# Joined score stretches, no copied left keys, no warm-up zeros, and a new written order in a fused attention and MLP kernel

## The chip, the cores and the metric

The kernel runs on one core of one Trainium2 chip. The metric is the device time of one execution in microseconds; a table below gives the runs of the kernel before. In the text PE is TensorE, DVE is VectorE, ACT is ScalarE, POOL is GpSimd and SP is SyncE, as in the profile.

## The reference

Banded attention with a linear bias by distance, and a squared-ReLU MLP on its output:

```
B, H, S, D = 4, 8, 768, 64         # d_model = 512, d_ff = 2048
scores = q @ k.T / sqrt(D)
keep   = (key < 8) or (0 <= query - key < 96)
scores = where(keep, scores - slope[h] * dist, -1e9)   # dist is 96 for a far global key
x   = softmax(scores) @ v          # rearranged to 3072 tokens x 512
h   = relu(x @ w_in)
out = (h * h) @ w_out              # fp32, 3072 x 512
```

## The kernel before

The 3072 tokens are 24 tiles of 128 rows (`j` = 0 to 23, six to a batch entry); two tiles make a block (`blk` = 0 to 11). A query of a tile sees only the keys of its own tile and of the one before, and the eight global keys; those are copied into the first eight columns of the left tile's keys and values (`gk`, `gv`). The first tile of a batch entry has no left tile and half the scores.

For a tile the steps are: `tr` and `T` (q and k transposed on PE and copied from PSUM) for tiles 0 to 7, or one DMA transpose `T` on SP from tile 8 on; `bias` (tiles 0 to 2 alone, a matmul that adds the bias); `sc` (the scores, matmuls of 64 rows, into two or four PSUM banks); `exp` on ACT, one for each bank; `mul` on DVE (by a table of the exponentiated bias and mask, from tile 3 on); `pv` on PE in two halves; `norm` on DVE (reciprocal and product); and `trx` with `xT` on PE and ACT or DVE, or `xT` by a DMA transpose from tile 8 on.

The MLP of block 0 is plain: `s1`, `relu`, `sq`, then `s2`, `o` and `st`. From block 1 (second layer) and block 2 (first layer) on it takes seven products in place of eight, in Strassen's manner: sums of inputs (`xs`), seven products `h` in three banks x, y and z, with the partial sums carried out of PSUM by `u` and added by `c`, squares `q`; then sums of the hidden values (`sum`), seven products `s2...p1` to `p7`, parts carried out by `part`, results `o` and stores `st`. `isum` and `wsum` make the sums of the two weight matrices once.

Nothing is scheduled at build time: `ORDER` is a written list of steps, and the instructions of all engines are issued in that order. A word names a step; `@A`, `@V` or `@P` after it puts it on ACT, DVE or POOL; digits after a colon are the PSUM banks, of eight, that the step opens; `#2` is the second step of the same name. Each engine runs its own steps in this order and waits for the data, the banks and the buffers that they need:

```
for word in ORDER.split():
    word, _, banks = word.partition(":")
    name, _, letter = word.partition("@")
    ...
    o["banks"] = [int(b) for b in banks]
```

The planner's costs, due times and dependences (`key`, `deps`, `takes`, `LEADS`, `SAFE`) are still in the code but issue nothing. The first loads (`ld.q.1`, `ld.win.3.0` and so on) and later ones (`load.j`: v, q and k of a tile) go through POOL's queue one after the other; q and k of tile 0, the DMA transposes and the stores go through SP's queue. Ahead of everything PE runs eight matmuls on zeros (L372), and between the transposes of q and of k of tile 0 a second eight (`warm`, L532).

For tiles 14, 15, 19, 20 and 22 (`COPY`), the keys that the next tile uses as its left keys are copied out whole, with the global keys, to a buffer `kl`; for the others `gk` writes the global keys in place after the tile's own scores. `JOIN` names tiles whose scores are emitted in the same step as those of the tile before; it is empty. In block 11 the last product `p3` is done in two cuts of 192 and 64 columns.

Of the kernel before, what the change touches and what calls it, by code (L numbers as in the profile page):

```python
# [57 lines left out]
tr.0.0:0 warm:7 tr.1.0:1 T.1.0@V bias.0.0:23 T.0.0@A sc.0.0 ld.win.3.0 exp.0.0.0 ld.k.1 tr.1.1:4 bias.1.0:5670 T.1.1@V ld.q.1  # L58
tr.0.1:1 ld.v.0 exp.0.1.0 T.0.1@V sc.1.0 exp.1.0.1 pv.0.0:2 ld.q.2 tr.0.2:3 norm.0.0 ld.k.2 T.0.2@V ld.k.3 exp.1.1.1
pv.0.1:4 tr.1.2:1 bias.2.0:7203 ld.v.1 norm.0.1 exp.1.1.0 ld.q.3 tr.1.3:6 gk.1@A T.1.2@A sc.2.0 exp.1.0.0 T.1.3@V  # L60
ld.k.4 pv.1.0:4 ld.v.2 gk.2@V exp.2.1.0 exp.2.1.1 norm.1.0 trx.0:1 xT.0@A ones.6 pv.1.1:5 tr.0.3:6 T.0.3@V exp.2.0.0
tr.1.4:2 ld.win.6.0 sc.3.0:4361 ld.q.4 norm.1.1 ld.v.3 trx.1:7 gv.1@V exp.2.0.1 exp.3.0.0 pv.2.0:5 exp.3.1.0 exp.3.0.1
T.1.4@V xT.1@V pv.2.1:0 ld.k.5 ld.win.2.0 exp.3.1.1 gk.3@A ld.win.2.1 norm.2.0 s1.0.3:2 mul.3.0 s1.0.6:4 ld.win.4.0
tr.0.4:7 ld.q.5 ld.v.4 norm.2.1 mul.3.1 relu.0.6@A s1.0.3#2 gv.2@P pv.3.0:3 norm.3.0 trx.2:5 T.0.4@A pv.3.1:6
ld.win.1.0 norm.3.1 ld.win.0.1 xT.2@A sc.4.0:1047 exp.4.1.1 exp.4.1.0 tr.1.5:3 T.1.5@A s1.0.2:5 trx.3:6 xT.3@V
ld.win.0.0 ld.win.5.0 s1.0.2#2 s1.0.2#3 s1.0.2#4 relu.0.3@V exp.4.0.1 ld.v.5 gv.3@P exp.4.0.0 gk.4@V sq.0.6@V
relu.0.2@A s1.1.3:7 ld.win.7.0 relu.1.3@A load.6 s1.1.6:0 mul.4.1 tr.0.5:6 mul.4.0 sq.0.3@V s1.1.2:3 T.0.5@A ld.wout.3
pv.4.0:2 ld.wout.1 sq.0.2@V sc.5.0:4157 ld.wout.0 s1.0.4:6 relu.1.2@A exp.5.1.1 s1.0.1:3 sq.1.3@A exp.5.0.0 relu.0.4@V
s1.1.4:7 ld.wout.2 norm.4.0 pv.4.1:4 gv.4@P norm.4.1 sq.0.4@A load.7 exp.5.1.0 sq.1.2@A relu.1.4@A s1.0.0:6 gate.9
ld.wout.4 mul.5.0 s1.0.0#2 sq.1.4@A s1.0.0#3 s1.1.5:2 trx.4:1 exp.5.0.1 relu.1.6@V s1.1.1:4 ld.wout.5 s1.0.1#2  # L70
relu.1.1@A E0.1 mul.5.1 relu.1.5@A pv.5.0:7 s1.1.7:0 s1.1.0:5 sq.1.1@V norm.5.0 ld.wout.6 E0.0 sq.1.5@V tr.1.6:4
sq.1.6@A pv.5.1:2 relu.1.7@A tr.0.6:7 s1.0.0#4 norm.5.1 xT.4@A sq.1.7@A h.2.0.p2:0 ld.wout.7 T.1.6@V h.2.1.p2:1
trx.5:2 xT.5@V relu.1.0@A sq.1.0@A gate.14 h.2.0.p1:5 xs.2.0 s1.0.5:4 sum.1.2 s1.0.7:2 relu.0.1@A xs.2.1 gate.10
sum.1.0 sum.1.1 relu.0.0@A T.0.6@A sc.6.0:36 wsum.0.0 sum.1.3 sq.0.0@A sq.0.1@A s2.0.0.0:7 relu.0.7@A s2.0.1.0 load.9
exp.6.0.0 xs.2.2 s2.0.2.0 exp.6.1.0 s2.0.3.0 s2.0.0.1:2 s2.0.1.1 wsum.2.0 relu.0.5@A sq.0.7@A s2.0.2.1 load.8 mul.6.0
wsum.1.0 s2.0.3.1 tr.0.7:3 tr.1.7:6 gate.15 isum.0.0 h.2.1.p1:4 T.0.7@A s2.0.4.0 isum.0.1 s2.1.p1.0:3 isum.3.1 T.1.7@A
sq.0.5@A pv.6.0:6 isum.1.1 s2.0.4.1 s2.0.5.1 u.2.0.1@A c.2.0.c11 s2.0.5.0 gate.11 u.2.1.1@A h.2.1.p6 q.2.0.c11@A
isum.1.0 T.8 s2.0.6.1 u.2.1.2@A s2.0.6.0 isum.3.0 pv.6.1:0 h.2.0.p6 wsum.2.1 wsum.0.1 s2.1.p1.1 s2.0.7.1 c.2.1.c11
norm.6.0 gate.13 o.0.1@V st.0.1 s2.0.7.0 h.2.1.p7 part.1.p1@A s2.1.p6.0 u.2.0.2@A o.0.0@A u.2.1.3@A h.2.0.p7 h.2.1.p4
T.9 norm.6.1 wsum.3.0 u.2.0.3@A sc.7.0:1762 c.2.1.c21@A wsum.1.1 h.2.1.p5:0 c.2.1.c22 q.2.1.c11@A s2.1.p2.0:4  # L80
exp.7.1.0 exp.7.0.0 isum.2.1 load.10 h.2.0.p4 exp.7.0.1 mul.7.0 exp.7.1.1 s2.1.p2.1 isum.2.0 s2.2.p1.0:7 q.2.1.c21@A
mul.7.1 h.2.0.p5:1 s2.1.p6.1 part.1.p6@A trx.6:6 gate.12 c.2.0.c21@A load.12 pv.7.0:2 xT.6@A c.2.0.c22 q.2.1.c22@A
q.2.0.c22@A s2.2.p1.1 h.2.1.p3 s2.1.p7.0 wsum.3.1 o.1.p2 norm.7.0 h.2.0.p3 pv.7.1:5 s2.1.p7.1 q.2.0.c21@A st.0.0
c.2.1.c12 s2.1.p5.0 s2.1.p5.1 part.1.p7@A q.2.1.c12@A s2.1.p4.0 T.10 s2.1.p4.1 c.2.0.c12 gk.7@V q.2.0.c12@A o.1.p5
o.1.p4@A sc.8.0:6201 st.1.1 part.2.p1@A s2.1.p3.0 norm.7.1 sum.2.0 sum.2.1 s2.1.p3.1 trx.7:5 xT.7@V o.1.p3 h.3.0.p1:3
exp.8.1.0 gk.8@V h.3.1.p1:2 exp.8.0.0 exp.8.1.1 exp.8.0.1 h.3.0.p2:6 xs.3.0 u.3.1.1@A sc.9.0:1540 s2.2.p6.0 mul.8.0
xs.3.1 mul.8.1 u.3.0.1@A h.3.0.p6 exp.9.0.1 exp.9.1.1 gv.7@V h.3.1.p2:4 c.3.0.c11 h.3.1.p6 c.3.1.c11 exp.9.0.0
pv.8.0:0 s2.2.p6.1 pv.8.1:6 load.11 norm.8.0 u.3.1.2@A s2.2.p2.0:1 sum.2.2 gv.8@P q.3.1.c11@A norm.8.1 xT.8 h.3.1.p7
h.3.0.p5:4 u.3.0.2@A h.3.0.p7 s2.2.p2.1 exp.9.1.0 st.1.0 part.2.p6@A xs.3.2 u.3.1.3@A q.3.0.c11@A h.3.1.p5:0 s2.2.p7.0
u.3.0.3@A mul.9.1 mul.9.0 s2.2.p7.1 c.3.1.c22 T.12 c.3.0.c22 pv.9.0:6 h.3.1.p3 o.2.p2 h.3.0.p4 c.3.1.c12 load.15  # L90
norm.9.0 q.3.1.c22@A h.3.0.p3 s2.3.p1.0:5 s2.3.p1.1 c.3.0.c12 q.3.0.c22@A pv.9.1:0 c.3.0.c21@A part.2.p7@A norm.9.1
q.3.1.c12@A h.3.1.p4 q.3.0.c12@A h.4.0.p1:3 c.3.1.c21@A s2.2.p5.0 part.3.p1@A gk.9@V sc.10.0:6402 s2.2.p5.1
q.3.0.c21@A sum.3.0 sum.3.1 s2.2.p4.0 s2.2.p4.1 exp.10.1.0 sum.2.3 exp.10.0.0 exp.10.0.1 h.4.0.p2:4 T.11 u.4.0.1@A
exp.10.1.1 gk.10@V gv.9@A s2.3.p6.0 o.2.p5 mul.10.0 c.4.0.c11 xT.9 h.4.1.p1:6 o.2.p4@A mul.10.1 s2.2.p3.0 s2.2.p3.1
q.3.1.c21@A s2.3.p2.0:0 sum.3.2 u.4.1.1@A pv.10.0:2 pv.10.1:4 s2.3.p6.1 xs.4.0 gate.17 o.2.p3 part.3.p6@A xs.4.1
s2.3.p2.1 norm.10.0 h.4.0.p6 h.4.1.p6 q.4.0.c11@A gv.10@A norm.10.1 u.4.0.2@A load.13 s2.3.p7.0 sc.11.0:7124 u.4.1.2@A
sum.3.3 h.4.0.p7 h.4.1.p7 xs.4.2 exp.11.1.0 o.3.p2 exp.11.0.0 u.4.0.3@V s2.3.p7.1 sc.12.0:17 exp.11.1.1 exp.11.0.1
gate.16 xT.10 h.4.0.p4 c.4.0.c21@A mul.11.0 st.2.0 mul.11.1 h.4.1.p2:4 c.4.1.c11 exp.12.1.0 s2.3.p5.0 pv.11.0:2
pv.11.1:3 s2.3.p5.1 norm.11.0 part.3.p7@A h.4.0.p5:7 q.4.1.c11@A u.4.1.3@A norm.11.1 h.4.1.p5:4 q.4.0.c21@A gate.20
s2.3.p4.0 c.4.0.c22 load.14 s2.3.p4.1 h.4.0.p3 T.13 gate.18 load.16 c.4.1.c22 exp.12.0.0 h.4.1.p4 q.4.1.c22@A h.4.1.p3  # L100
xT.11 s2.4.p2.0:2 h.5.0.p1:3 q.4.0.c22@A o.3.p5 mul.12.0 c.4.0.c12 o.3.p4@A c.4.1.c21@A u.5.0.1@A c.4.1.c12 T.15
s2.3.p3.0 q.4.0.c12@A s2.3.p3.1 q.4.1.c12@V q.4.1.c21@A h.5.0.p2:1 o.3.p3 sc.13.0:5764 st.3.1 st.2.1 h.5.1.p1:0
exp.13.0.0 T.14 s2.4.p2.1 c.5.0.c11 exp.13.1.0 pv.12.1:1 q.5.0.c11@A s2.4.p1.0:5 xs.5.0 sum.4.0 pv.12.0:7 xs.5.1
s2.4.p1.1 mul.13.0 h.5.0.p6 gk.13@V u.5.1.1@A exp.13.0.1 h.5.1.p6 exp.13.1.1 h.5.0.p5:6 sum.4.1 norm.12.0 norm.12.1
h.5.1.p2:4 xs.5.2 mul.13.1 c.5.1.c11 h.5.1.p5:7 u.5.1.2@A sum.4.2 gate.19 part.4.p1@A h.5.1.p7 u.5.0.2@A h.5.0.p7
o.4.p2 u.5.0.3@A c.5.0.c22 pv.13.0:1 u.5.1.3@A norm.13.0 s2.4.p6.0 s2.4.p6.1 xT.12 st.3.0 q.5.1.c11@A T.16 part.4.p6@A
h.5.0.p4 pv.13.1:4 s2.4.p5.0 sum.4.3 c.5.0.c21@A h.5.0.p3 h.5.1.p4 q.5.0.c22@A s2.4.p7.0 norm.13.1 s2.4.p7.1 s2.4.p5.1
c.5.0.c12 q.5.0.c21@A kl.15@V part.4.p7@A c.5.1.c22 q.5.0.c12@A sc.14.0:1346 o.4.p5 s2.4.p4.0 xT.13 exp.14.0.1 kl.14@V
h.5.1.p3 gv.13@P q.5.1.c22@V c.5.1.c12 c.5.1.c21@A s2.4.p4.1 load.17 h.6.0.p1:4 s2.4.p3.0 s2.4.p3.1 exp.14.1.1
exp.14.1.0 exp.14.0.0 sc.15.0:0673 mul.14.1 mul.14.0 xs.6.0 o.4.p4@A xs.6.1 h.6.0.p2:1 o.4.p3 q.5.1.c12@A s2.5.p1.0:5  # L110
u.6.0.1@A c.6.0.c11 exp.15.0.0 exp.15.1.0 exp.15.1.1 sum.5.0 s2.5.p1.1 h.6.0.p6 u.6.0.2@A exp.15.0.1 sum.5.1 load.18
h.6.0.p5:2 part.5.p1@A pv.14.0:0 norm.14.0 pv.14.1:6 h.6.1.p1:1 u.6.1.1@A h.6.0.p7 gv.14@P st.4.0 s2.5.p6.0 u.6.0.3@A
# [1319 lines left out]
```

## Time and profile before

| | |
|---|---|
| runs, us | 199.13, 199.85, 200.0 (median 199.85) |
| profiled execution, us | 199.37 |
| its span, us | 197.6 |
| instructions in the span | 6777 |
| DVE busiest groups | `c` sums L995 (45 + 15), products L690 (39), norms L779 (48) |
| ACT busiest groups | squares L1015 (72), exponentials L665 (78 + 10), `u` copies L429 (42 + 15) |
| loads by POOL's queue | 24 of v, 23 each of q and k, 10 pieces of w_in, 8 of w_out |

The span runs from the first to the last instruction of the core; the execution's own time is 1.8 us longer. A group is the instructions of one line, engine and form; its mean is the time of one from start to end, and instructions of one engine overlap a little, so that the distance from start to start is shorter than that mean. A chain piece gives the time that the chain spends in a run of instructions of one line.

### The profile page before, as it was taken

To read this page: it belongs to the slowest core of one execution; us is meant where nothing else is said; L and a number is where in the kernel's file an instruction comes from. 1 tells how busy PE (TensorE), PEld (TensorE's weight loads), DVE (VectorE), ACT (ScalarE), POOL (GpSimd) and SP (SyncE) were. 2 spreads that over 40 slices of the span, in tenths; PEclk is the share of its full clock that TensorE was granted. 3 is DMA by queue.
4 is the path that set the end of the run, shared out by engine and by line. 5 is a ranking of instruction groups with operands and counts; after the bars stand their busy time and mean duration, and the time that the engine had idled before them with its cause. 6 is when DMAs were issued, how large, how long until landed. Compare 5 with 4: busy or idle time off the path is not lost.

```text
span 197.6 us, 6777 instructions
## 1 busy us (share of the span) xinstructions
PE 191.9 (97%) x2776; PEld 169.6 (86%) x2776; DVE 173.2 (88%) x423; ACT 163.0 (82%) x335; POOL 80.4 (41%) x101
## 2 busy tenths in 40 slices
...
GB/s 127 153 158 171 181 181 185 182 202 159 139 209 191 75 200 88 145 174 210 151 129 203 114 124 194 160 121 92 136 81 116 154 55 56 27 30 163 0 106 106
DMA packets 111857, 26.91 MB, mean 136 GB/s; under 512 B 103379, under 2 KB 109011, under 8 KB 111827
## 3 DMA queue, kind: packets, MB, share of 16 engines
...
q8 instruction: 21, 0.34, 0.6%
...
## 4 chain that ended last, share of the span: by engine, by line
PE 95%; DVE 2%; issue 1%; ACT 0%; DVEq 0%
PE bank L1212 35%; PE bank L950 32%; PE bank L1061 7%; PE bank L599 6%; PE bank L748 5%; PE bank L1339 4%; PE bank L372 2%; PE bank L506 2%; PE bank L532 1%; DVE qkT L433 1%; PE bank L816 1%; PE bank L579 0%; ACT qkT L429 0%; DVE o L1287 0%; DVE v L433 0%
## 5 line engine op out<-in xcount | busy, mean ns | idle before, releaser
L1015 ACT ACTIVATE hs<-hr 128x512 bf16<-128x512 f32 x72 | 44.8, 641 | 5.1 <-DVE hr L995 4.7
L665 ACT ACTIVATE esc<-bank 128x512 bf16<-128x512 f32 x78 | 42.9, 614 | 1.3 <-PE bank L599 1.0
L1212 PE MATMUL bank<-wsum,hsum 128*128 128x256 bf16 x264 | 36.2, 273 | 0.0
L1212 PEld LDWEIGHTS <-hsum 128*128 128x128 bf16 x360 | 32.1, 98 | 4.1 <-issue 0.5
L995 DVE CUSTOM_DVE_ANT_0 hr<-bank,early 128x512 f32<-128x512 f32 x45 | 30.4, 685 | 2.5 <-PE bank L950 1.5
L950 PEld LDWEIGHTS <-win 128*128 128x128 bf16 x480 | 29.7, 98 | 1.0
L950 PEld LDWEIGHTS <-qk_first 128*128 128x128 bf16 x480 | 29.7, 98 | 1.0
L429 ACT COPY early<-bank 128x512 f32<-128x512 f32 x42 | 24.5, 591 | 3.6 <-PE bank L950 3.3
L690 DVE TENSOR_TENSOR at<-esc,E 128x1024 bf16<-128x1024 bf16 x39 | 26.7, 696 | 0.1
L1212 PEld LDWEIGHTS <-hs 128*128 128x128 bf16 x264 | 24.0, 98 | 2.6
L310 POOL DMA_DIRECT2D qk<-in_q_dram x18 | 16.0, 890 | 21.9 <-DMA qkT<-qk 20.6
L1212 PE MATMUL bank<-wout,hs 128*128 128x256 bf16 x176 | 24.9, 273 | 0.0
L310 POOL DMA_DIRECT2D v<-in_v_dram x18 | 16.0, 888 | 18.3 <-DVE v L480 14.9
L950 PE MATMUL bank<-xT,win 128*128 128x128 bf16 x320 | 23.4, 219 | 0.0
L431 POOL COPY v<-v 8x520 bf16<-8x520 bf16 x8 | 5.7, 718 | 43.3 <-PE bank L748 43.3
L950 PE MATMUL bank<-xs,qk_first 128*128 128x128 bf16 x320 | 22.8, 219 | 0.0
L779 DVE TENSOR_TENSOR x<-bank,rs 128x256 bf16<-128x256 f32 x48 | 20.4, 425 | 1.7
L865 ACT ACTIVATE hr<-bank 128x512 f32<-128x512 f32 x33 | 19.4, 598 | 1.3 <-PE bank L950 0.4
L748 PE MATMUL bank<-v,at 128*128 128x65 bf16 x352 | 17.8, 193 | 0.0
L1287 DVE TENSOR_TENSOR o<-bank,part 128x256 f32<-128x256 f32 (+2 forms) x34 | 13.8, 410 | 3.3 <-PE bank L1212 3.2
L429 ACT COPY part<-bank 128x256 f32<-128x256 f32 x29 | 10.9, 375 | 7.1 <-PE bank L1212 6.9
L310 POOL DMA_DIRECT2D qk<-in_k_dram x18 | 16.1, 897 | 0.9 <-DMA win<-in_moe_w_in_dram 0.5
...
## 6 DMA issues: line engine op xcount, KB each, us to landing
out_dram<-o SPq DMA_DIRECT2D x22, 256.0 KB, 2.5
...
wout<-in_moe_w_out_dram POOLq DMA_DIRECT2D x8, 256.0 KB, 8.5
win<-in_moe_w_in_dram POOLq DMA_DIRECT2D x6, 256.0 KB, 6.9
...
```

Source lines behind the costliest of these rows:

```text
L310: nc.gpsimd.dma_start(out=dst, in_=src)
L429: nc.scalar.copy(dst, src)
L665: nc.scalar.activation(out=tiles[tag, j, g][:, odd], in_=tiles.pop(("sc", j, odd, g)).rearrange("p a c -> p (a c)"), func=Act.Exp, scale=s ...
L690: nc.vector.tensor_mul(at, tiles.pop(("esc", j, g)), bias)
L748: nc.tensor.matmul(out=po[:, hi, :], lhsT=tiles["at", j, g][:, odd, at * P : (at + 1) * P], rhs=v_sb[kj][:, h, :], start=(i == 0), stop=(i ...
L779: nc.vector.tensor_tensor(out=x[:, 4 * hf : 4 * hf + 4, :], in0=po[:, :, :D], in1=rs.to_broadcast([P, 4, D]), op=Alu.mult,)
L865: nc.scalar.activation(dst, src, Act.Relu)
L950: nc.tensor.matmul(out=tiles["h", blk, g, bank][:, n], lhsT=left_[:, s, k], rhs=right_[:, k], start=opens and n == 0 and k == 0, stop=k == ...
L995: nc.vector._custom_dve(TENSOR_ADD_SAT, out=hr, in0=src, in1=tiles.pop(("u", blk, g, i)), s0=float("inf"), s1=0.0,)
L1015: nc.scalar.activation(hs, hr, Act.Square)
L1061: nc.tensor.matmul(out=hT[:, c, cols], lhsT=w_in_sb[s][:, kt, c * P : (c + 1) * P], rhs=tiles["xT", blk][:, kt, cols], start=(kt == 0), st ...
L1212: nc.tensor.matmul(out=tiles["acc", blk, bank][:, cols], lhsT=left_[:, s], rhs=right_[:, cols], start=first and s == 0, stop=s == NSTEP - ...
```

## The change

Seven things differ; all the rest of the code is the same.

- `JOIN` holds tiles 7, 13 and 19: their scores are emitted in the step of tiles 6, 12 and 18, and that step opens six banks (`sc.6.0:751063`: the first two for tile 6, the other four for tile 7). 21 score steps are left of 24.
- `COPY` is empty: no `kl` step, five more `gk` steps.
- The second eight matmuls on zeros are gone.
- The buffers of `u` are taken from a list of free ones, not in turn.
- `pv` names the load of the left tile's values as a dependence (for the planner).
- In block 11 both cuts of `p3` are entered as done with the last matmul, and the order has both adds behind all matmuls.
- `ORDER` is new in whole. On POOL's queue q of tile 1 is now first, then k of tile 1 (before: a piece of w_in, then k, then q); the pieces of w_in and `v` of tile 5 come after most q, k and v, and tiles 6 and 7 are loaded ahead of w_out. Loads and DMA transposes stand in groups of their own.

```diff
-    JOIN = set()
-    COPY = [14, 15, 19, 20, 22]
+    JOIN = {(7,0),(13,0),(19,0)}
+    COPY = []
...
-    NKEEP = 8
...
-        if j == 0:
-            def emit_warm(e):
-                for _ in range(NKEEP):
-                    nc.tensor.matmul(out=psum(), lhsT=zero[:, :P], rhs=zero, start=True, stop=True)
-
-            plan.op(("warm",), {"PE": 0.216 * NKEEP}, emit_warm, key=base)
...
-        def open_sc(gs, j=j):
-            for n, (g, odd) in enumerate((g, odd) for g in gs for odd in range(2)):
+        def open_sc(gs, at=0, j=j):
+            for n, (g, odd) in enumerate(((g, odd) for g in gs for odd in range(2)), at):
...
-        def emit_sc(e, gs, j=j, todo=todo, open_sc=open_sc):
+        def emit_sc(e, gs, at=0, j=j, todo=todo, open_sc=open_sc):
             if isinstance(gs, list):
                 for f, gs in gs:
-                    f(e, gs)
+                    f(e, gs, at)
+                    at += 2 * len(gs)
                 return
...
-                deps.append(glob.get(("v", j - 1)))
+                deps += [glob.get(("v", j - 1)), land["v", j - 1]]
...
-    u_next = [0]
+    u_free = list(u_ring)
...
-                    u = u_ring[u_next[0] % NU]
-                    u_next[0] += 1
+                    u = u_free.pop(0)
...
+                        u_free.append(u)
...
-                for o, cols in zip(done, cuts):
+                for o, cols in zip([done[-1]] * len(cuts), cuts):
```

Of the new order, the parts that the text speaks of. The start, up to the first step of the MLP (POOL's loads and the other engines' steps stand in one list):

```
ld.q.1 ld.k.1 ld.v.0 ld.k.2 ld.q.2 ld.v.1 ld.q.3 ld.k.3 ld.q.4 ld.v.2 ld.k.4 ld.k.5 ld.v.3 ld.win.3.0 ld.q.5 ld.v.4
ld.win.0.0 ld.win.1.0 tr.0.0:0 T.0.0@V ones.6 load.6 ld.win.0.1 ld.win.2.0 ld.win.2.1 ld.v.5 ld.win.6.0 ld.win.4.0
ld.win.7.0 ld.win.5.0 load.7 ld.wout.0 ld.wout.1 ld.wout.2 ld.wout.3 ld.wout.5 ld.wout.4 ld.wout.6 ld.wout.7 tr.1.0:1
T.1.0@A bias.0.0:23 tr.0.1:4 sc.0.0 exp.0.1.0 exp.0.0.0 tr.1.1:5 T.0.1@V T.1.1@V bias.1.0:6701 sc.1.0 gate.9 gk.1@V
pv.0.0:4 norm.0.0 exp.1.0.0 pv.0.1:3 exp.1.0.1 tr.1.2:5 norm.0.1 T.1.2@V bias.2.0:2640 tr.0.2:3 exp.1.1.0 pv.1.0:7
norm.1.0 exp.1.1.1 trx.0:5 pv.1.1:1 gv.1@V norm.1.1 xT.0@V T.0.2@A sc.2.0 exp.2.1.0 exp.2.0.1 tr.0.3:3 tr.1.3:7 gk.2@A
T.0.3@V T.1.3@V exp.2.0.0 trx.1:1 tr.0.4:6 sc.3.0:5437 pv.2.0:2 exp.2.1.1 pv.2.1:0 exp.3.0.1 xT.1@V exp.3.0.0 norm.2.0
gk.3@V gv.2@V T.0.4@V tr.1.4:1 norm.2.1 T.1.4@A exp.3.1.0 mul.3.0 tr.1.5:3 sc.4.0:2516 exp.3.1.1 exp.4.0.0 trx.2:4
mul.3.1 pv.3.0:0 pv.3.1:7 exp.4.1.0 norm.3.0 norm.3.1 s1.0.3:2 exp.4.0.1 gk.4@A s1.0.3#2 trx.3:5 tr.0.5:0 exp.4.1.1
gv.3@V mul.4.0 mul.4.1 pv.4.0:1 xT.2@V pv.4.1:7
```

The joined score steps and what is ahead of them, and a stretch of block 11:

```
s2.0.0.0:3 ... s2.0.7.0 wsum.2.0 o.0.0@A st.0.0 T.11 c.2.1.c11 s2.0.4.1 sc.6.0:751063
s2.2.p4.1 o.2.p4@A h.4.1.p6 o.2.p3 xT.10 st.2.0 st.2.1 sum.3.0 u.4.1.2@A sc.12.0:304726
sc.17.0:1325 s2.4.p4.1 gate.22 load.22 sum.5.2 exp.17.0.0 exp.17.0.1 exp.17.1.1 sum.5.0
sum.5.1 o.4.p4@A s2.4.p3.1 s2.5.p1.0:1 c.6.0.c12 o.4.p3 exp.17.1.0 h.6.1.p4 mul.17.1 c.6.1.c21@A sc.18.0:205673
h.11.0.p7 s2.10.p6.0 s2.10.p6.1 q.11.0.c11@A u.11.1.2@V sum.10.3 sum.10.2 u.11.0.3@V
c.11.0.c22 part.9.p7@A h.11.1.p7 sum.9.3 s2.10.p2.1 s2.9.p4.0 o.9.p5 q.11.0.c22@A h.11.0.p3
```

And the last steps, before and after:

```
s2.11.p3.0 s2.11.p3.1 s2.11.p3.0#2 o.11.p3 s2.11.p3.1#2 st.11.0#2 o.11.p3#2 st.11.0#3      # before
s2.11.p3.0 s2.11.p3.1 ... s2.11.p3.0#2 s2.11.p3.1#2 o.11.p3 st.11.0#2 o.11.p3#2 st.11.0#3  # after
```

204 lines of the change are left out of this document (97 added, 107 removed).

## The prediction

> **What bounds the kernel now.** I read the page first: busy times, then the chain that ended last.
>
> ```profile
> span 197.6 us, 6777 instructions
> PE 191.9 (97%) x2776; PEld 169.6 (86%) x2776; DVE 173.2 (88%) x423; ACT 163.0 (82%) x335; POOL 80.4 (41%) x101
> PE 95%; DVE 2%; issue 1%; ACT 0%; DVEq 0%
> ```
>
> The chain is TensorE (PE) for 95% of the span, and VectorE (DVE) is close behind with 88% busy. So the next question is where PE waits. The list of waits has these lines for PE's matmuls, and asked for 40 to 193 us alone it has none:
>
> ```profile
> PE bank L372 <- DVE early L361: 1.2, 1, 1.2
> PE bank L599 <- DVE qkT L433: 1.1, 3, 0.5
> PE bank L1212 <- DVE o L1287: 0.5, 1, 0.5
> ```
>
> From 40 us to the last step the old order therefore keeps PE fed without one wait. A new order can gain there only by less PE work, and it loses whatever wait it brings in. The chain in order of time, and the timeline of the same place, show the one thing there that is not work:
>
> ```profile
> 18.29 1.32 PE bank L1061 x16
> 19.83 0.45 PE bank L1061 x8
> 42.55 0.45 PE bank L506 x8
> 84.21 0.49 PE bank L748 x16
> 140.69 0.55 PE bank L599 x16
> 141.24 0.55 PE bank L950 x8
> 141.79 0.44 PE bank L1212 x4
> 142.23 0.45 PE bank L950 x8
> ```
>
> ```profile
> 140.69 0.22 PE L599 MATMUL bank<-qkT,kl 64*128 64x128 bf16 x2
> 140.74 0.22 PE L599 MATMUL bank<-qkT 64*128 64x128 bf16 x2
> ```
>
> A product of eight matmuls (L950) takes 0.45, but 0.55 right behind a stretch of scores (L599). The sixteen score matmuls start in pairs 0.055 apart, 8 x 0.055 = 0.44, yet the stretch takes 0.55. So each stretch costs 0.10 going in and 0.10 coming out. The other rows give PE's prices: four transposes (L506) 0.22, a `pv` (L748) 0.25, half an `s2` step (L1212) 0.44; a matmul itself lasts 0.22 from start to end.
>
> **The change part by part.** The base is the profiled execution: 199.37 us, with a span of 197.6; the median of the runs is 199.85, and 0.5% of it, about what a measurement of this kernel can tell, is 1.0 us.
>
> *Joined stretches.* Tiles 6+7, 12+13 and 18+19 go in one stretch each, so three changes in and out go: 3 x 0.2 = -0.6.
>
> *Copies, small edits.* The five `kl` copies fall away, and five narrow `gk` copies take their place, on ACT and DVE. PE waits for neither, so this is worth 0; should it be the cover of a late step, some tenths. The free list for `u` and the planner's extra dependences add no instruction. No PE wait in the list names a key tile transposed by DMA, so keeping loads and transposes apart has nothing to give PE: 0.
>
> *Start: no zeros, loads in another order.*
>
> ```profile
> 1.19 3.60 PE L372 MATMUL bank<-early 128*128 128x512 bf16 x8 [1.19 <-DVE early L361]
> 1.25 0.56 SPq L319 DMA_DIRECT2D plain<-in_k_dram  x1
> 1.34 0.89 POOL L307 DMA_DIRECT2D win<-in_moe_w_in_dram  x1 [0.17 <-issue]
> 2.22 0.90 POOL L307 DMA_DIRECT2D qk_first<-in_k_dram  x1
> 5.43 2.62 PE L532 MATMUL bank<-early 128*128 128x512 bf16 x8
> 7.89 0.60 PE L506 MATMUL bank<-ident,plain 128*128 128x128 f32 x4
> 9.71 1.09 ACT L665 ACTIVATE at<-bank 128x512 bf16<-128x512 f32 x2 [3.44 <-PE bank L599]
> 11.62 0.23 PE L599 MATMUL bank<-qkT 64*128 64x128 bf16 x2 [0.52 <-DVE qkT L433]
> 17.31 2.12 ACT L665 ACTIVATE esc<-bank 128x512 bf16<-128x512 f32 x4
> 18.12 1.49 PE L1061 MATMUL bank<-xT,win 128*128 128x128 bf16 x16
> ```
>
> ```profile
> plain<-in_k_dram SPq DMA_DIRECT2D x1, 256.0 KB, 6.0
> win<-in_moe_w_in_dram POOLq DMA_DIRECT2D x6, 256.0 KB, 6.9
> ```
>
> The zeros (L532) end at 8.05, but k of tile 0, issued at 1.25, lands 6.0 later, at 7.25. They hide that wait and hold the next transposes up by 0.6 at most (7.89 against 7.3). The first exponentials, now at 9.71, then come 0 to 0.6 earlier; I take 0, as scores still wait for copy and bias.
>
> What is late next is the first step of the MLP, `s1.0.3`, at 18.12 now. In the new order it stands behind `pv.3.1` on PE, and thus behind all fourteen exponentials of tiles 0 to 3 on ACT. Two of them take 1.09 and four 2.12, so 0.5 each and the last about 0.6. From 9.7: 13 x 0.5, two copies `T` and a `gk` ahead (about 1.2) is 17.4; the waits for `sc.1.0` and `sc.2.0`, which no longer overlap with other work, I put at 1.1; so the last starts at 18.5 and ends at 19.1, and its `mul` (0.7, row further down) and `pv` (0.25) bring `s1.0.3` to 20.2. The weight is not sooner: `ld.win.3.0` goes from first to fourteenth on POOL's queue, 1.34 + 13 x 0.88 + 6.9 = 19.7. By 20.2 the old order has done three steps of `s1` (L1061 in the chain, 1.32 + 0.45 = 1.8 us of PE); the new one has instead the scores of tile 4, one transpose, one `trx` and one `pv` more, 1.3. Behind by 0.45. Then `pv.4.0` and `pv.4.1` stand behind `mul.4.1`, again four exponentials on, another 0.45 (0 to 0.9). Of the loads behind, `load.6` with its three DMAs goes ahead of most `win` pieces: `ld.win.0.1`, now twenty-second, lands at 1.34 + 21 x 0.88 + 6.9 = 26.7, about when PE comes to it (26.5 with the delays so far). Together +0.9, between 0 and 1.6. On SP stores go behind transposes; none frees a buffer that PE waits for.
>
> A rule of the Trainium skill bears on the zeros ("TensorE: Matmul & The Clock Gate", Part 1): the array runs at half rate until a window of about 3.4 us of activity has passed. The trace agrees: the first eight matmuls of 512 columns take 3.60, the second eight 2.62, so the rate changed within them. By the rule, PE idle from 5.4 to 7.3 could leave the start cold; the first rival below prices this.
>
> *Tail.*
>
> ```profile
> 194.16 0.36 DVE L1287 TENSOR_TENSOR o<-bank,part 128x192 f32<-128x192 f32 x1 [0.84 <-PE bank L1212]
> 194.57 0.28 PE L1212 MATMUL bank<-wout,hsum 128*128 128x64 bf16 x4 [0.45 <-DVE o L1287]
> 194.88 0.22 DVE L1287 TENSOR_TENSOR o<-bank,part 128x64 f32<-128x64 f32 x1 [0.37 <-PE bank L1212]
> ```
>
> The last matmul of the block before ends just ahead of 194.16, and PE starts 0.05 after the add ends at 194.52: such a handing on costs 0.05. The last four matmuls no longer wait 0.45 for the first add; both adds now follow all matmuls, so the first add and its store come 0.1 later and the second 0.3 earlier at best, behind the first store's issue on SP: -0.1 (-0.3 to 0.1).
>
> *What the joined stretches ask for.* A joined stretch opens six of the eight banks at once. The rows for the instructions that free them, and DVE's pace:
>
> ```profile
> L429 ACT COPY o<-bank 128x512 f32<-128x512 f32 x1 | 0.6, 585 | 0.0
> L429 ACT COPY o<-bank 128x256 f32<-128x256 f32 x10 | 3.8, 377 | 3.6 <-PE bank L1212 3.5
> L690 DVE TENSOR_TENSOR at<-esc,E 128x1024 bf16<-128x1024 bf16 x39 | 26.7, 696 | 0.1
> 46.36 0.68 DVE L888 TENSOR_TENSOR plain<-win 128x1024 bf16<-128x1024 bf16 x1
> 46.96 0.68 DVE L1132 TENSOR_TENSOR wsum<-wout 128x1024 bf16<-128x1024 bf16 x1
> 58.32 0.42 DVE L1287 TENSOR_TENSOR o<-bank,part 128x256 f32<-128x256 f32 x1
> 58.66 0.17 DVE L778 RECIPROCAL rs<-bank 128x4 f32<-128x4 f32 x1
> 58.87 0.42 DVE L779 TENSOR_TENSOR x<-bank,rs 128x256 bf16<-128x256 f32 x1
> 59.21 0.68 DVE L1167 TENSOR_TENSOR hsum<-hs 128x1024 bf16<-128x1024 bf16 x1
> ```
>
> `sc.18.0:205673` takes bank 3, which `sc.17.0` filled and `exp.17.1.0` empties. Between the two PE has three steps of `s2` and one `h`, 4 x 0.44 = 1.8. ACT has, 0.2 after the scores' end, three exponentials (1.5), `o.4.p4` (0.38 or less; 0.3), then the one wanted, 0.6: 2.6. PE stands for 0.8, more if ACT comes late: 0.9 (0.8 to 1.1). `sc.12.0:304726` takes bank 6, emptied by `o.2.p4` on ACT, whose source `s2.2.p4.1` is the last but one step on PE: 0.22 + 0.38 + 0.05 against one `h` of 0.45 is 0.2, and `exp.11.0.1` and `part.3.p1` stand ahead on ACT: 0.5 (0.2 to 0.65). `sc.6.0:751063` takes bank 3 of `s2.0.7.0`, emptied by `o.0.0`: 0.22 + 0.59 + 0.05 against `s2.0.4.1`, 0.43: 0.4 (0.2 to 0.45). Sum +1.8, between 1.2 and 2.2: the joining costs three times what it saves.
>
> *DVE from `sc.6.0` to `sc.10.0`.* With tile 7 pulled in, its products and norms meet six `wsum`. Up to and with `c.3.0.c11`, which frees bank 7 for `sc.10.0:2107`, DVE has 21 instructions of the long kind, 0.60 from start to start (46.36, 46.96): 12.6; six norms of 0.55 (58.66 to 59.21): 3.3; three `o` of 0.34: 1.0; `xs`, `gk`, gate 0.9: 17.8 in all. PE has 11 `h`, 19 `s2`, 6 `pv`, 2 `trx` and three stretches of scores: 4.9 + 8.3 + 1.2 + 0.4 + 2.3 = 17.1. DVE is late by 0.8 if it never waits itself, and it must wait for some `pv`; less what the wait at `sc.6.0` already gave: +0.9 (0.4 to 1.8).
>
> *The rest of the order.* Near the end `h.11.0.p3` waits for `c.11.0.c22`, behind `u.11.1.2`, two sums and `u.11.0.3`, now on DVE: 5 x 0.6 + 0.1 against five PE steps, 2.2: +0.8 (0 to 0.9). In all the letters move six `u`, seven `part` and three `q` from ACT to DVE, some 9 us for the engine that was already at 88%. Seven more places (`sc.15.0`, `s2.4.p2.0`, `s2.4.p3.0`, `sc.20.0`, `sc.21.0`, `pv.21.0`, `sc.23.0`) have the consumer 0.2 to 0.4 too close by the same count, 2.1 together; a delay met earlier takes up part of them, so +0.9 (0 to 2.2).
>
> Sum: -0.6 - 0.1 + 0.9 + 1.8 + 0.9 + 0.8 + 0.9 = +4.6; 199.4 + 4.6 = 204.0. With the low ends: -0.6 - 0.3 + 0 + 1.2 + 0.4 + 0 + 0 = +0.7; with the high ends -0.6 + 0.1 + 1.6 + 2.2 + 1.8 + 0.9 + 2.2 = +8.2.
>
> **The rivals.** *Cold start, 205.5.* If the array runs at half rate from 7.3 until about 11, the PE work ahead of the second tile's scores (two fp32 transposes' worth, biases, two stretches, about 3.2 us) doubles, ACT starves and `s1.0.3` slips by about 1.5. For it: the idle gap that replaces L532. Against it: the work after 7.3 is nearly dense itself. Chance 0.15.
>
> *The waits melt, 200.7.* The waits are not added but overlap: once PE is late, DVE and ACT have caught up, and only the longest counts. Then -0.7 + 0.9 from the start and 1.1 for the longest: +1.3. Against it: three of them hang on a PE step just ahead, which a delay moves along. Chance 0.15; about half of it is within 1.0 us of no change.
>
> *Faster, 197.7.* q and k of tile 1 lead the queue, so `sc.1.0`, at 11.6 now, follows 1.0 sooner, and PE keeps this lead: -0.7 - 1.0 = -1.7. It decides if `s1.0.3` starts before 19.0 and PE shows no wait past 40 us. Against it: the fourteen exponentials. Chance 0.05.
>
> *Not what it says.* On POOL's queue q of tile 1 stands before its k, against the description. Scores need both, so it moves nothing: no case of its own.
>
> **How the numbers follow.** Forecast 0.6, near 204; cold start 0.15; melted 0.15; faster 0.05; elsewhere 0.05. The range 200.7 to 206.5 leaves out the fast case, half the melted one and the top of the sum. Slower by over 0.5%: 0.6 + 0.15 + 0.08 + 0.03 = 0.86; within: 0.09; faster: 0.05.
>
> **What would show it.** PE waits at the three joined stretches named, by ACT, of 0.4 to 0.9; a wait by DVE ahead of `sc.10.0`; `s1.0.3` at about 20; score stretches down to 21; DVE busier than 173 us, ACT less than 163. It is wrong if the list of PE's waits past 40 us is again empty.

## The result, and the profile after

The changed kernel takes 202.31 us (median of four runs, 202.05 to 203.18) where the kernel before took 199.62 beside it: a ratio of 1.0147, 95% interval 1.0117 to 1.0178. It is slower by 2.7 us; the forecast of 204.0 had the side right and was 1.7 too high. Ratios, here and below, leave out a few slower runs of some kernels, medians do not. The profiled execution of after took 202.39 for a span of 200.6, against 199.37 and 197.6, so its 3.0 us more are what there is to place.

The page of after, its busy times and its chain:

```profile
span 200.6 us, 6768 instructions
PE 191.8 (96%) x2768; PEld 169.1 (84%) x2768; DVE 180.8 (90%) x441; ACT 151.9 (76%) x311; POOL 80.9 (40%) x102
PE 48%; DMA 22%; POOL 14%; DVE 8%; issue 3%; ACT 2%; SPq 1%; DVEq 0%; POOLq 0%; ACTq 0%
```

PE has as much work as before. DVE went up by 7.6 us and ACT down by 11.1, as the letters said. What changed is the chain: PE carried 95% of it before, and 48% now, with 36% on transfers and on POOL, which issues the loads. The list of PE's waits, asked for 40 to 198 us, is no longer empty:

```profile
PE bank L593 <- DMA qkT<-qk: 1.3, 3, 0.9
PE bank L1205 <- DVE hr L989: 0.3, 1, 0.3
PE bank L944 <- DVE hr L989: 0.2, 1, 0.2
```

Scores (L593) wait three times for a key tile that a transfer transposes (`T.j` in the order). The chain in order of time shows what stands behind two of them:

```profile
43.77 7.38 DMA qk<-in_k_dram
51.23 4.44 DMA qkT<-qk
55.72 0.67 PE bank L593 x16
...
81.17 4.93 DMA v<-in_v_dram
86.10 0.97 SPq L530
87.17 1.25 SPq L530
88.47 0.57 SPq L1374
89.15 6.34 DMA qkT<-qk
95.53 0.62 PE bank L593 x16
```

`sc.8` at 55.72 follows the landing of `T.8`, which follows the landing of its load. `sc.15` at 95.53 follows `T.15`, which stood on SP's queue behind two other transposing transfers and the store `st.0.1` (L1374). The timeline shows what the waits come to, and a joined stretch that did not wait:

```profile
55.72 0.23 PE L593 MATMUL bank<-qkT 64*128 64x128 bf16 x2 [0.18 <-DMA qkT<-qk]
78.75 0.45 PE L593 MATMUL bank<-qkT 64*128 64x128 bf16 x10 [0.24 <-DMA qkT<-qk]
95.53 0.23 PE L593 MATMUL bank<-qkT 64*128 64x128 bf16 x2 [0.92 <-DMA qkT<-qk]
114.67 0.45 PE L593 MATMUL bank<-qkT 64*128 64x128 bf16 x10
115.12 0.33 PE L593 MATMUL bank<-qkT 64*128 64x128 bf16 x2
```

The start, first in the list of transfers (the last number is the time to landing), then in the timeline:

```profile
plain<-in_k_dram SPq DMA_DIRECT2D x1, 256.0 KB, 3.8
```

```profile
7.10 1.09 ACT L659 ACTIVATE at<-bank 128x512 bf16<-128x512 f32 x2 [0.49 <-PE bank L593]
18.52 1.05 PE L1054 MATMUL bank<-xT,win 128*128 128x128 bf16 x16
```

k of tile 0 came 3.8 after its issue and not 6.0, the first exponentials at 7.10 and not 9.71, yet the first step of the MLP at 18.52, later than the 18.12 of before.

To see where time goes when the order itself is new, lay the matmuls of both kernels in their order and count each at the spacing of its shape in a gapless run (0.22 for 512 columns, 0.11 for 256, 0.055 for 128; two half-array matmuls 0.055), the zeros left out. Both come to 178.4 us of work. The start of the matmul at the same amount of work, after less before:

```
work done  1     7     11    36    48    60    84    156   168   176   last   end of span
t before   9.4   17.8  22.1  47.7  60.1  72.4  97.3  171.6 183.6 191.7 194.7  197.6
after less -3.0  -3.4  -0.6  -0.3  +0.8  +0.9  +2.3  +2.0  +3.0  +3.0  +2.4   +3.0
```

The new order is ahead at first, has lost nearly all of that lead at 22 us, and then loses in three places: 1.2 around `sc.8` and `sc.9` (work 43 to 48), 1.4 from `sc.12` to `sc.15`, and 1.0 in blocks 9 to 11.

### The profile page after: what moved, and what is told of

Read it like the earlier page. It is cut to its first block, busy times and chain, and to the rows that moved or that the text cites. A ratio compares the mean times of both kernels' runs of the same rounds, so it can differ in the third digit from the quotient of the medians.

```text
span 200.6 us, 6768 instructions
## 1 busy us (share of the span) xinstructions
PE 191.8 (96%) x2768; PEld 169.1 (84%) x2768; DVE 180.8 (90%) x441; ACT 151.9 (76%) x311; POOL 80.9 (40%) x102
## 4 chain that ended last, share of the span: by engine, by line
PE 48%; DMA 22%; POOL 14%; DVE 8%; issue 3%; ACT 2%; SPq 1%; DVEq 0%; POOLq 0%; ACTq 0%
PE bank L1205 23%; PE bank L944 19%; DMA qkT<-qk 7%; DMA wout<-in_moe_w_out_dram 5%; POOL qk_first L306 4%; DMA win<-in_moe_w_in_dram 4%; DMA qk<-in_k_dram 4%; POOL win L306 3%; PE bank L593 3%; PE bank L742 3%; POOL v L306 3%; DVE hr L989 3%; DMA v<-in_v_dram 2%; POOL qk L309 2%; DVE hsum L1160 2%
## 5 line engine op out<-in xcount | busy, mean ns | idle before, releaser
L1008 ACT ACTIVATE hs<-hr 128x512 bf16<-128x512 f32 x69 | 43.3, 642 | 14.7 <-DVE hr L989 14.4
L659 ACT ACTIVATE esc<-bank 128x512 bf16<-128x512 f32 x78 | 43.7, 610 | 4.3 <-PE bank L593 3.4
L428 ACT COPY early<-bank 128x512 f32<-128x512 f32 x38 | 22.3, 590 | 6.0 <-PE bank L944 4.4
L944 PE MATMUL bank<-xs,qk_first 128*128 128x128 bf16 x320 | 23.7, 219 | 0.0
L859 ACT ACTIVATE hr<-bank 128x512 f32<-128x512 f32 x30 | 18.1, 603 | 4.7 <-DVE hs L1093 3.1
L742 PEld LDWEIGHTS <-at 128*128 128x128 bf16 x352 | 15.1, 98 | 2.5 <-DVE at L684 1.6
L1054 PE MATMUL bank<-xT,win 128*128 128x256 bf16 (+1 forms) x160 | 15.9, 251 | 0.0
```

The costliest lines, as they stand in the source:

```text
L428: nc.scalar.copy(dst, src)
L659: nc.scalar.activation(out=tiles[tag, j, g][:, odd], in_=tiles.pop(("sc", j, odd, g)).rearrange("p a c -> p (a c)"), func=Act.Exp, scale=s ...
L742: nc.tensor.matmul(out=po[:, hi, :], lhsT=tiles["at", j, g][:, odd, at * P : (at + 1) * P], rhs=v_sb[kj][:, h, :], start=(i == 0), stop=(i ...
L859: nc.scalar.activation(dst, src, Act.Relu)
L944: nc.tensor.matmul(out=tiles["h", blk, g, bank][:, n], lhsT=left_[:, s, k], rhs=right_[:, k], start=opens and n == 0 and k == 0, stop=k == ...
L1008: nc.scalar.activation(hs, hr, Act.Square)
```

## The experiments

Each ratio is to the kernel before on the same chip. "Lag" is the number of the table above for the run's own profile: its time less that of before at equal PE work. Some profiles lack the records of three matmuls, which are then counted in.

**Where the scores stand.** One reading of the two traces carries most of what follows. Before, the answers on the tile `qkT`, for the transfers `T.8` and `T.12` alone and, in the last row, for the four issued between 80 and 100 us, of which `T.15` is one (their issue, then issue to landing; `T.15`'s own landing is not in the trace):

```profile
L537 SPq DMA_TRANSPOSE qkT<-qk x1: 1337/1337/1337, 51.5 to 51.5; - x1
DMA to landing us min/median/max: 3.7/3.7/3.7
...
L537 SPq DMA_TRANSPOSE qkT<-qk x1: 1294/1294/1294, 69.3 to 69.3; - x1
DMA to landing us min/median/max: 4.1/4.1/4.1
...
DMA to landing us min/median/max: 4.6/6.5/7.4
```

The timeline of before, with `sc.8`, `sc.12`, `T.15` and `sc.15`:

```profile
59.03 0.23 PE L599 MATMUL bank<-qkT 64*128 64x128 bf16 x2
82.37 0.40 PE L599 MATMUL bank<-qkT 64*128 64x128 bf16 x8
87.89 1.25 SPq L537 DMA_TRANSPOSE qkT<-qk  x1
103.91 0.23 PE L599 MATMUL bank<-qkT 64*128 64x128 bf16 x2
```

`T.8` lands at 51.5 + 3.7 = 55.2 and is used at 59.0: 3.8 us in hand. `T.12` lands at 69.3 + 4.1 = 73.4, used at 82.4: 9.0. `T.15`, issued at 87.9 and used at 103.9, has 8.6 even if it took the slowest one's 7.4. In after all three have nothing in hand. Part of that is the transfers: `T.15` is issued 1.3 later (89.15), `T.12` over 4 later (73.9) and lands 5.3 later, at 78.7. `T.8` is not issued later (51.49 before, 51.23 after; in all fourteen profiles 50.9 to 52.0) and lands 0.5 later. The rest is that the scores are asked for sooner: in PE work done, `sc.8` stands at 43.8 in place of 47.1, `sc.12` at 64.9 in place of 69.5, `sc.13` at 64.9 in place of 77.2, `sc.15` at 80.2 in place of 90.3. This is the larger part for `sc.8` and `sc.15`; for `sc.12` the later transfer is.

How closely the scores then follow, the profiles of the new order show together. There are ten, those of run 3 to run 10 and of run 12 beside that of after, and `T.8` lands in them between 55.6 and 59.6 us. In nine `sc.8` starts 0.05 after that landing; in the tenth (run 5) PE itself came later. `sc.12` starts 0.05 behind `T.12` in seven, `sc.15` 0.05 behind `T.15` in six.

**1. Before without the zeros.**

```diff
-tr.0.0:0 warm:7 tr.1.0:1 T.1.0@V
+tr.0.0:0 tr.1.0:1 T.1.0@V
```

> The kernel before with the eight matmuls on zeros (L532) taken out and nothing else changed. Theory, the loads hold the start: k of tile 0 still lands at about 7.25, so the first exponentials stay within 0.6 of 9.71 and the time within 0.6 of before: 199.0 to 199.6. Rival, the zeros hold the start: first exponentials at about 7.1 as in the kernel after, 197 or less. Rival, cold array: the transposes and biases after the gap run at half rate, first exponentials later than 9.9 and a time of 200.5 or more.

Measured 200.10 against 199.34, ratio 1.0035 (1.0007 to 1.0062). None of the three expectations fits whole: the exponentials came 2.0 earlier, against the first, and the time did not follow them, against the second. In the profile k of tile 0 took 3.9 to land, with the loads in the order of before, and the first exponentials came at 7.71; so the 6.0 of the first profile was that execution's own, and the late start is not a matter of load order. Where the lead of 2.0 went, in the timeline of this run:

```profile
17.67 1.05 PE L1055 MATMUL bank<-xT,win 128*128 128x256 bf16 x8 [1.13 <-DMA win<-in_moe_w_in_dram]
105.58 0.62 PE L944 MATMUL bank<-xs,qk_first 128*128 128x128 bf16 x8 [0.43 <-DVE xs L916]
```

1.1 went to a weight's load; a lead of 0.8 then stood unchanged from 22 to 101 us, and 0.6 of it went where DVE waited for a transposed x that came at the same time as in before. A lead of PE was worth nothing here where the next transfer did not move with it.

**2. The same, with q, k and v of tile 1 ahead of the first weights.**

```diff
-... T.0.0@A sc.0.0 ld.win.3.0 exp.0.0.0 ld.k.1 ... ld.q.1
+ld.q.1 ld.k.1 ld.v.0 ld.win.3.0 tr.0.0:0 tr.1.0:1 ...
```

> The kernel before without the zeros, and with q, k and v of tile 1 ahead of the first weights of the MLP on POOL's queue (four words of the order moved); the rest of the order is that of before. Theory, the order of the loads and the zeros together make the early start: k of tile 0 lands at about 5, first exponentials at about 7.1. If PE then bounds the rest, as it did in before from 22 us on, the lead of 2.6 stays and the time is 197.0 (196.6 to 197.6). Rival, weights and exponentials take it back between 10 and 22 us, as in the kernel after: s1.0.3 within 0.5 of 18.1 and 199.0 to 199.6.

Measured 199.85, ratio 1.0021 (0.9992 to 1.0050): the rival's time, though not its place, for `s1.0.3` came at 16.49 and not near 18.1. Lag -2.2 at first, -0.8 at 22 us, +0.4 at the end; 1.1 of that went at 106 us, where DVE's `xs` held PE for 0.9.

**3. After with the zeros put back.**

```diff
-ones.6 ... tr.0.0:0 T.0.0@V
+ones.6 ... tr.0.0:0 warm:7 T.0.0@V
```

> The kernel after with the eight matmuls on zeros put back behind tr.0.0, as in before. They end at about 8.05, so the first exponentials come at about 9.7 in place of 7.1. Theory, the lead of the start is lost between 10 and 22 us whatever its size, since loads and ACT set s1.0.3: s1.0.3 within 0.8 of 18.5 and a time of 202.3 to 203.0. Rival, the lead is carried to the end: 204.9.

Measured 204.13, ratio 1.0226 (1.0188 to 1.0264), beside 1.0147 for after. Neither number fits whole. The zeros took 1.89 here and not 2.62, and the start was later by 1.05 than in after (lag -2.0 against -3.0); of that, 0.76 was left at 22 us and 0.04 at `sc.15`. There after stood waiting for `T.15`, and this run came without a wait, at the same time:

```profile
56.41 0.45 PEld L600 LDWEIGHTS <-qkT 64*128 64x128 bf16 x16 [0.42 <-DMA qkT<-qk]
95.57 0.23 PE L600 MATMUL bank<-qkT 64*128 64x128 bf16 x2
```

At `sc.8` (the first row) it waited as after did, as `T.8`, issued when it was in after, landed 0.7 later, at 56.37. So the late start did not reach the end. This run is 0.93 behind after at 192 us because it lost 0.9 anew between 99.6 and 105.9, in pauses of which the trace puts two down to DVE and ACT; why these were late was not followed further.

**4. After with 28 small steps of DVE on ACT.**

```diff
-q.2.0.c11@V ... part.6.p6@V ... u.11.0.3@V ... part.11.p7@V
+q.2.0.c11@A ... part.6.p6@A ... u.11.0.3@A ... part.11.p7@A
```

> The kernel after with 28 small steps (u, part and q of all blocks) taken from DVE to ACT, where before had all but one of them; the order of the steps is that of after. Theory, DVE is the bound of the late waits: DVE busy about 166 in place of 181, the pauses of PE at 175.4 and 183.4 (0.5 each) and the one of 0.3 at 58.2 gone, 201.1 to 201.4. Rival, DVE is not what they wait for, or ACT becomes late in its place: 202.3 or more.

Measured 206.41, ratio 1.0352 (1.0317 to 1.0387): the rival, and by 4 us. DVE fell to 167.9 busy, ACT rose to 163.0, and PE now waited for ACT's copies, by the list of waits from 22 us on:

```profile
PE bank L1205 <- ACT part L428: 1.8, 2, 1.5
PE bank L944 <- ACT early L428: 1.0, 2, 0.5
```

DVE at 90% is no fault by itself: taken together, the letters fit this order.

**5. After with `T.15` and `T.12` sooner on SP.**

```diff
-xT.9 T.13 T.12 ... T.14 T.16 load.17 st.0.1 T.15 xT.12
+xT.9 T.12 T.13 ... T.14 T.15 T.16 load.17 st.0.1 xT.12
```

> The kernel after with two steps moved on SP's queue: the transposing transfer T.15 ahead of T.16, load.17 and the store st.0.1, and T.12 ahead of T.13. Theory, sc.15 waits 0.9 for a transfer that is queued too late, and sc.12 0.25 for one too: both waits go, 201.1 to 201.4. Rival, DVE or ACT is as late there and the waits only change their name: 202.0 or more.

Measured 203.41, ratio 1.0185 (1.0152 to 1.0218): the rival. PE's list of waits from 40 us on names no transfer any more. The wait at `sc.12` had moved inside the joined stretch, though: `T.13`, now second, landed at 79.24, and the scores of tile 13 start at 79.29, their weight load 0.21 late. And from 60 to 84 us of work the lag grew by 1.4 (1.4 to 2.8), as much as in after. Within `sc.14` and behind `sc.15` PE paused 0.3 to 0.35 each; DVE, from which it waited, had itself stood, in its timeline:

```profile
90.12 0.43 DVE L916 TENSOR_TENSOR xs<-xT 128x512 bf16<-128x512 bf16 x1 [0.85 <-DMA xT<-x]
```

That is a transfer of the same kind (`xT`, the transposed x) on the same queue. It was issued 0.3 later than in after, ahead of the moved `T.15`, and landed 1.9 later (90.09 against 88.17); whether the moved ones made it slower was not separated.

**6. After with the joined stretches taken apart.**

```diff
-sc.6.0:751063 h.2.1.p7 ... s2.0.5.1
+sc.6.0:75 h.2.1.p7 ... s2.0.5.1 sc.7.0:1063
-sc.12.0:304726 ... s2.3.p6.0
+sc.12.0:30 ... s2.3.p6.0 sc.13.0:4726
-sc.18.0:205673 s2.5.p1.1
+sc.18.0:20 s2.5.p1.1 sc.19.0:5673
```

> The kernel after with the three joined stretches taken apart: the scores of tiles 7, 13 and 19 come one or two PE steps behind those of tiles 6, 12 and 18, with the banks they had. Theory, a stretch waits bank by bank, so joining asked for almost nothing and saved three changes in and out: +0.6, 202.9, less up to 0.3 for the pauses at the joined stretches. Rival, as predicted, the six banks at once cost 1.8 and the splitting gives it back: 201.1.

Measured 203.35, ratio 1.0193 (1.0152 to 1.0233) against after's 1.0147 (1.0117 to 1.0178). The rival's gain of 1.2 is excluded; a loss of 0.6 fits, though the two intervals overlap.

**7. After with five late steps on ACT.**

```diff
-part.9.p1@V ... q.10.1.c22@V ... part.10.p1@V ... u.11.1.2@V ... u.11.0.3@V
+part.9.p1@A ... q.10.1.c22@A ... part.10.p1@A ... u.11.1.2@A ... u.11.0.3@A
```

> The kernel after with five steps near the end alone taken from DVE to ACT (part.9.p1, q.10.1.c22, part.10.p1, u.11.1.2, u.11.0.3). Theory, DVE back to back holds PE at 175.4 and 183.4 and ACT has room there: both pauses of about 0.4 over the normal spacing go, 201.4 to 201.8. Rival, as in the run with 28 letters, ACT becomes late in its place: 202.3 or more.

Measured 202.73, ratio 1.0147 (1.0108 to 1.0186), no gain that the time shows. In the trace the later of the two pauses is gone. Two of the five steps on DVE (the copies to `u` and `early`) and what waited behind them, in after, and then PE in this run:

```profile
180.64 0.68 DVE L432 COPY u<-bank 128x512 f32<-128x512 f32 x1
182.44 0.69 DVE L432 COPY early<-bank 128x512 f32<-128x512 f32 x1
183.16 0.69 DVE L989 CUSTOM_DVE_ANT_0 hr<-bank,early 128x512 f32<-128x512 f32 x1
183.91 0.61 PE L944 MATMUL bank<-xT,qk_first 128*128 128x128 bf16 x8 [0.21 <-DVE hr L989]
```

```profile
175.06 0.61 PE L944 MATMUL bank<-xT,qk_first 128*128 128x128 bf16 x8 [0.28 <-DVE hr L989]
182.82 0.60 PE L1205 MATMUL bank<-wsum,hs 128*128 128x256 bf16 x4
183.26 0.61 PE L944 MATMUL bank<-xT,qk_first 128*128 128x128 bf16 x8
```

`h.11.0.p3` (183.91 in after, 183.26 here) follows its forerunner without a gap, but the pause at 175 stays. From 156 to 168 us of work the lag grew by 0.7, against 0.9 in seven profiles without this edit: 0.2 of the hoped 0.8.

**8. After with `c.2.1.c22` ahead of the norms on DVE.**

```diff
-... h.2.1.p5:6 wsum.1.1 norm.6.1 norm.7.0 ... s2.1.p5.1 c.2.1.c22
+... h.2.1.p5:6 wsum.1.1 c.2.1.c22 norm.6.1 norm.7.0 ... s2.1.p5.1
```

> The kernel after with one step moved on DVE: c.2.1.c22, which frees bank 4 for sc.8, ahead of the norms of tiles 6 and 7. Theory, DVE holds sc.8 although the profile names a transfer: the pause of 0.34 ahead of sc.8 at 55.3 goes and the exponentials of tile 8 come as much sooner, 201.7 to 202.1. Rival, the transfer named by the profile: the pause stays, 202.3.

Measured 203.15, ratio 1.0161 (1.0125 to 1.0198). The pause ahead of `sc.8` stayed, 0.26 where after had 0.34, with the weight load of the scores waiting for the transfer:

```profile
56.28 0.54 PEld L593 LDWEIGHTS <-qkT 64*128 64x128 bf16 x16 [0.38 <-DMA qkT<-qk]
```

`T.8` landed at 56.24 and `sc.8` started at 56.28, so the releaser that the profile named was the true one. My reading against it had the wrong owner: bank 4 is read last by `c.2.1.c21` on ACT.

**9 and 10. After with loads and transfers sooner, without and with the five late steps on ACT.**

```diff
-    NQ, NKT, NV = 3, 2 * TPB, 10
+    NQ, NKT, NV = 4, 2 * TPB, 10
-load.10 load.11 T.10 ... T.11 ... gv.7@P ... gv.8@P load.12 load.14 ... T.13 T.12 ... load.15 ... T.14 T.16 ... T.15
+load.10 load.11 T.10 T.11 load.12 load.13 ... gv.7@P load.14 ... T.12 T.13 st.1.0 st.1.1 ... gv.8@P load.15 ... xT.8 T.14 xT.9 T.15
```

> The kernel after with the loads and the transposing transfers of tiles 11 to 15 taken apart no longer: four buffers for arriving q and k in place of three, the loads of tiles 12 to 15 sooner on POOL's queue, T.11 to T.15 sooner on SP's. The order on PE, ACT and DVE is that of after (but for four tiny marks on DVE). Theory, the new order asks for scores sooner than loads and transfers in batches can deliver: the waits ahead of sc.12 and sc.15 (0.25 and 0.9 in the profile of after, 1.1 to 1.2 together in its variants) go and DVE's wait for xT.11 does not come, 201.0 to 201.5. Rival, ACT and DVE are as late there, and something else holds PE by as much: 202.2 or more. The pauses at sc.8 and sc.9 stay under both, since T.8 cannot go before its load lands at 51.

> The run before this one with the five late steps on ACT as well. Theory, the two causes lie apart and add: 0.3 less than that run, 200.7 to 201.2. Rival, what one gives the other takes: the same as that run.

Measured 217.16, ratio 1.0811 (1.0746 to 1.0875), and 215.44, ratio 1.0698 (1.0639 to 1.0757). Neither theory nor rival foresaw it: it cost 13 to 15 us beside after. Run 10 is below run 9 by more than 0.3, but both scatter over 4 to 5 us, so whether the causes add stays open. PE's waits of run 9 from its timeline, and the wait of DVE behind one of them:

```profile
58.80 0.23 PE L593 MATMUL bank<-qkT 64*128 64x128 bf16 x2 [3.24 <-DMA qkT<-qk]
81.02 0.62 PE L742 MATMUL bank<-v,at 128*128 128x65 bf16 x8 [5.06 <-DVE at L684]
125.60 0.23 PE L593 MATMUL bank<-qkT 64*128 64x128 bf16 x2 [4.11 <-DMA qkT<-qk]
...
79.94 0.42 DVE L1280 TENSOR_TENSOR o<-bank,part 128x256 f32<-128x256 f32 x1 [5.33 <-DMA out_dram<-o]
```

Two waits for transposed keys, and one for a store that stood behind `T.12` and `T.13` on SP and held an `o` buffer.

**11. Before without the zeros, with two places filled.**

```diff
-... ld.k.4 ... ld.v.2 ... ld.win.6.0 ... h.6.0.p6 ... h.6.0.p5:2 ... pv.14.0:0 norm.14.0 pv.14.1:6
+... ld.win.6.0 ld.k.4 ... ld.v.2 ... pv.14.0:0 h.6.0.p6 ... pv.14.1:6 h.6.0.p5:2 ... norm.14.0
```

> The kernel before without the zeros, with the load of ld.win.6.0 ahead of ld.k.4, and with pv.14.0 and pv.14.1 ahead of two h steps of block 6. Theory, the two places where the run without zeros gave its lead back (1.1 at the second s1 step for that load, 0.4 at 105 us for a transposing transfer) are filled: a lead of 1.0 to 1.8 stays to the end, 197.8 to 198.6. Rival, the transfers come at their own times whatever PE does, and another wait takes the place: 199.3 or more.

Measured 200.55, ratio 1.0048 (1.0017 to 1.0078): the rival. A load of k that came behind the moved one now held PE for 1.6 at 15.8 us, and a transposed x for 0.6 at 106.

**12. After with four buffers for arriving q and k.**

```diff
-    NQ, NKT, NV = 3, 2 * TPB, 10
+    NQ, NKT, NV = 4, 2 * TPB, 10
```

> The kernel after with one size changed: four buffers for arriving q and k in place of three; the order of all steps is that of after. The loads of tile 11 then need not wait for the transposing transfer T.8 and run beside T.8 to T.10, and so on down the queue. Theory, a load beside a transposing transfer makes it slower: T.8 takes 7 to 8 us in place of 4, sc.8 waits about 3 us, and the time is 204.5 to 206. Rival, the run with the moved loads lost its time by the stores and transfers that were moved on SP, not by the overlap: T.8 lands as in after and 202.0 to 202.7.

Measured 213.71, ratio 1.0653 (1.0581 to 1.0724): the theory at `sc.8`, and about three times its price, or more, in all. One number, no step moved, 10 us by the ratios and 11.5 by the profiles. The answer on the tile for `T.8` here, and in the timeline the scores behind it and a second such wait:

```profile
L530 SPq DMA_TRANSPOSE qkT<-qk x1: 1892/1892/1892, 51.7 to 51.7; - x1
DMA to landing us min/median/max: 7.7/7.7/7.7
```

```profile
59.40 0.23 PE L593 MATMUL bank<-qkT 64*128 64x128 bf16 x2 [3.10 <-DMA qkT<-qk]
122.36 0.23 PE L593 MATMUL bank<-qkT 64*128 64x128 bf16 x2 [4.12 <-DMA qkT<-qk]
```

`T.8` is issued when it was (51.7 against 51.2) and takes 7.7 to land in place of 4.4: q and k of tile 11, which after issues at 56.2 and 57.1, no longer wait for it and are issued at 49.7 and 50.6. Three transfers around 112 us (`T.19`, `T.17`, `T.18`) took 7.6, 10.1 and 8.5, where the same three took 6.2, 5.7 and 5.2 in after. So a transposing transfer beside more loads landed 1 to 4 us later, and the ring of three buffers, by making the load of tile j+3 wait for `T.j`, is what keeps the two apart. PE's waits for such transfers add up to 9.9 in this run's list, against 1.3 in after.

## Why the prediction was right, and where its steps were not

The side was right, for reasons of which half were. That the total came within 1.7 us is in part luck: 1.8 for the joined stretches, which did not come, stood in for the waits on transfers, put at 0. The terms against the table of lag:

```
step of the prediction                      forecast   measured in the profile after
start, to 22 us                              +0.9       -0.6
to sc.9 (sc.6 joined 0.4, DVE 0.9, -0.2)     +1.1       +1.5  (work 11 to 48)
sc.12 to sc.15 (joined 0.5, -0.2, one seventh of 0.9)
                                             +0.4       +1.4  (work 60 to 84)
to block 9 (sc.18 joined 0.9, -0.2, six sevenths of 0.9)
                                             +1.5       -0.3  (work 84 to 156)
blocks 9 to 11                               +0.8       +1.0  (work 156 to 168)
last steps                                   -0.1        0.0  (-0.6, then +0.6)
sum                                          +4.6       +3.0
```

(The 0.9 of the seven further places is shared out evenly, `sc.15` being one of them. The measured entries are rounded; of the 1.5, 0.3 came ahead of `sc.6`. Three small sums of the prediction are off by a tenth or so: 17.8 less 17.1 is 0.7, 3.1 less 2.2 is 0.9, and 19.1 with 0.7 and 0.25 is about 20.1.)

*Loads and transposes apart: 0.* This is the step that failed. I argued that no PE wait in the list of before names a key tile transposed by transfer. An empty list says that nothing is late, not by how much it is early. What was wanted was the margin, 3.8 us at `sc.8` and 9 at `sc.12` and `sc.15`, and beside it how much sooner the new order asks. That sum was to be had blind from the trace of before and the order. In after PE's list has 1.3 us of waits at these three, each ended by a landing 0.05 before. And the separation is not worth 0: run 12 lost 10 us by weakening it. It was there before as well, since the ring of three gave it; what is new is that scores follow their transfers with nothing in hand. No run won the time back: run 5 took most of these waits away and others came in their place, so what their removal alone is worth stays open.

*Start: +0.9.* The size and the sign failed. k of tile 0 was taken as landing at 7.25, from one execution; in the others that I looked at it took 3.8 to 5.3 from its issue. Fourteen exponentials ahead of `s1.0.3` was the right reading, but they began 2.6 earlier, and `s1.0.3` came at 18.52 in place of 20.2. What holds is that the start decides little: 11 us of PE work are done between 21.3 and 22.3 us in all fourteen profiles, with first exponentials from 7.0 to 9.7, and in run 3 what was left of a late start was gone at `sc.15`.

*Joined stretches: -0.6, and +1.8 for six banks at once.* The saving fits run 6. The cost does not: a joined stretch waits bank by bank inside itself, so bank 3 of `sc.18` is wanted 0.45 after the stretch's start (the row at 115.12, where the pause within the stretch is 0.06), and the exponential that empties it ends at 115.19:

```profile
114.54 0.65 ACT L659 ACTIVATE esc<-bank 128x512 bf16<-128x512 f32 x1
```

Of the predicted 0.9, 0.5 and 0.4 for `sc.18`, `sc.12` and `sc.6`, none came by ACT.

*DVE from `sc.6.0` to `sc.10.0`: +0.9.* The place and the size came out, the cause did not: `sc.8` waited for `T.8` (the landings above, and run 8), and `sc.9` and the transpose behind it paused 0.27 each until exponentials of tile 8 on ACT had emptied their banks. DVE was back to back there, 19.8 us busy of the 20 from 40 to 60, but so it had been before (19.7), without holding PE. At `sc.10.0`, where the count had led, PE paused under 0.1.

*`h.11.0.p3` behind DVE: +0.8.* The place and the cause were right, and run 7 shows them; the size was not: this pause is 0.3 to 0.4 (183.91 in after). The rest of the 1.0, most of it at 175, was not foreseen.

*Tail: -0.1.* The wait of 0.45 on PE went, and the end came 0.6 later behind the last matmul (3.6 after its start, 2.95 before). No net change, as said.

*Copies and small edits: 0.* Nothing contradicts it; it was not tested alone.

Of the rivals, the cold start did not come: matmuls of after run at full spacing from 5.8 us on without the zeros. What a gap can do to the clock was seen elsewhere, in the granted clock (PEclk) of two stretches of run 12:

```profile
core 0: us, PE busy (x) PEld busy (x) DVE busy (x) ACT busy (x) POOL busy (x), PEclk, DMA share, GB/s
55.00:62.00 7.00, 3.90 (x63) 3.11 (x62) 4.19 (x12) 2.27 (x5) 1.24 (x2) 1.00 1.46 198
116.00:126.00 10.00, 5.75 (x60) 4.36 (x58) 5.11 (x12) 5.08 (x10) 3.15 (x4) 0.83 1.49 142
```

With a wait of 3.10 the clock stayed at 1.00, with one of 4.12 it fell to a mean of 0.83. The Trainium skill, "TensorE: Matmul & The Clock Gate", section "Why this matters for your kernels", asks for no idle gaps of TensorE over about 3 us; these rows agree. No pause at the start of after comes near that. "The waits melt" holds for one stretch, work 84 to 156, where 1.5 was forecast and none came. "Faster" had named its condition as `s1.0.3` before 19.0 and no wait past 40 us; the first half was met, the second not. Of the signs that the prediction named, the three waits by ACT, the wait ahead of `sc.10.0` and `s1.0.3` at 20 did not come; a busier DVE, an idler ACT and a list of waits that is not empty did.
